# A scan followed by a mixture of adapters: from per-batch phases to one pipeline over units of 512 tokens, with 2 KB runs and part of the gating on GpSimd

## The chip, the cores and the metric

The kernel runs on one core of a Trainium2 chip. The metric is device time in microseconds (us); lower is better. Every run quoted gave the correct result. PE is the matmul engine (PEld its weight loads), DVE is VectorE, ACT is ScalarE, POOL is GpSimd, and SP is the engine that only issues transfers. GB/s is what the core's 16 DMA engines moved. L12 is line 12 of the kernel that the trace belongs to.

## The reference

```
a, b: (8 batches, 6400 steps, 128 channels) fp32
h[t] = a[t] * h[t-1] + b[t]            # per batch and channel, h starts at 0
x = all h as (51200 tokens, 128)
logits = x @ w_gate                    # 8 experts
top 2 experts of each token, weights = softmax over those two
out = x + sum over the two: weight * (x @ A[e]) @ B[e]     # rank 16
```

The two inputs are 26.2 MB each, and so is the output: 78.6 MB of transfers.

## The kernel before

Time runs along the free dimension in the scan, so tokens are transposed in: PE transposes 128x128 fp32 blocks of `a` and `b` into PSUM, ACT copies the transposed `a` to SBUF, and DVE scans 512 tokens at once into `xT` (fp16). Then come logits, gating, `Z = x A`, the gated multiply `zw` on DVE, its transpose, a copy on ACT, the delta matmuls (with `x` added through an identity), the copy out on ACT, and the store.

```
# loads: a whole batch of a, then of b; a run in DRAM is one token, 512 B
sp.dma_start(a_tm[slot][:, :, :], a[bi].rearrange("(j p) d -> p j d", p=128))
sp.dma_start(b_tm[slot][:, :, :], b[bi].rearrange("(j p) d -> p j d", p=128))

# stores, on GpSimd's queue, 512 B runs
pool.dma_start(out[r0:r1, :].rearrange("(j p) d -> p j d", p=128), outt[...])

# order on DVE for each batch k: scans of batch k+1 alternate with multiplies of batch k,
# then the gating of the whole next batch at once
for ci in range(NCH):
    emit_scan(bA, ci + 1); emit_Zw(bZ, ci)
emit_scan(nA, 0); emit_scan(nA, 1)
emit_gating(bA)     # ten dependent DVE operations on 128x400, two sigmoids on ACT between
... (cut)
```

## Time and profile before

| | before |
|---|---|
| time, median of the first 3 runs | 304.25 us (304.02 to 305.71) |
| PE, DVE, ACT busy | 74%, 74%, 57% |
| first scan starts | 28.5 us |
| 512 tokens when fed (128 to 137 us) | 1.88 us on PE, 1.77 us on DVE |
| one batch (78.6 MB / 8 = 9.83 MB of traffic), mid-run | 31.2 us |

The page of the profile has one line of totals, then one digit for each fortieth of the span (busy tenths; 9 means 90% or more), then the GB/s of each fortieth.

```profile
PE 224.9 (74%) x2800; PEld 208.9 (69%) x2800; DVE 224.5 (74%) x290; ACT 172.4 (57%) x330; POOL 80.7 (27%) x113
...
PE   0014993599959996899599877988599859974871
...
DVE  0001892899879987998889787988799889968430
...
DMA  6999999998599989997999889998999641444364
GB/s 194 269 291 289 290 292 290 289 291 252 158 360 327 326 287 353 336 300 238 331 351 292 308 253 353 310 345 241 353 315 342 197 121 37 141 144 117 106 203 125
```

In order: the totals, then PE, DVE, the DMA engines and GB/s by slices. No engine is full, and the holes in PE and DVE recur with a period: one per batch. The timeline of DVE shows such a border (start, length, engine, line, operation, and in brackets the idle time before it and what ended it):

```profile
146.52 1.28 DVE L437 TENSOR_TENSOR_SCAN xT<-a_st,xT,pqB 128x512 f16<-128x512 f32 x1
...
148.03 0.58 DVE L449 COPY L<-pL 128x400 f32<-128x400 f32 x1 [0.23 <-PE pL L248]
...
151.56 0.21 DVE L487 TENSOR_TENSOR d<-m 128x50 f32<-128x50 f32 x1
153.39 0.57 DVE L491 TENSOR_TENSOR t<-mask,w 128x400 f32<-128x400 f32 x1 [1.62 <-ACT w L360]
...
155.15 0.69 DVE L526 TENSOR_TENSOR zw<-pZ,g 128x512 f16<-128x512 f32 x1
```

The lines shown are the last scan before the border, the first and the last step of the gating before the sigmoids, the first step after them, and the first multiply of the next batch. From 147.8 us, when the last scan before it ends, until 155.15 us, when the first multiply of the next batch begins, DVE works at gating, or waits for ACT. Part of that wait comes from the stores: in ACT's order the sigmoid stands behind copies out, two of which had waited for a store just before (1.47 us until 149.25 us, 1.25 us until 151.35 us). At the border near 247 us, where no copy waited for a store, DVE waited 0.45 us for the sigmoid instead of 1.62. Counting from first multiply to first multiply, 123.95 to 155.15 us, a batch takes 31.2 us, of which its 12.5 pairs of scan and multiply need 12.5 x 1.77 = 22 us.

The waits list gives who waited for whom: us in total, number of times, longest.

```profile
DVE xT L437 <- PE pqB L231: 24.1, 5, 17.2
...
ACT outt L378 <- DMA out_dram<-outt: 22.9, 16, 2.9
```

### The profile page before, as it was taken

How to read it: one execution, taken by the hardware profiler on the slowest of the kernel's cores; microseconds unless marked ns; L12 is line 12 of the kernel's file. 1: busy time of each engine (PE TensorE's matmuls, PEld its weight loads, DVE VectorE, ACT ScalarE, POOL GpSimd, SP SyncE). 2: the span in 40 equal slices, each digit the busy share in tenths (PEclk: the TensorE clock that was granted, in tenths of full speed). 3: DMA queues.
4: the chain of work that ended last, by engine and by line, in shares of the span. 5: the costliest groups of instructions: out<-in, count | busy, mean ns of one | idle time of the engine just before them, and what ended most of it. 6: DMA issues, size and time to landing. Idle time of an engine off the chain costs nothing.

```text
span 304.2 us, 7139 instructions
## 1 busy us (share of the span) xinstructions
PE 224.9 (74%) x2800; PEld 208.9 (69%) x2800; DVE 224.5 (74%) x290; ACT 172.4 (57%) x330; POOL 80.7 (27%) x113
## 2 busy tenths in 40 slices
PE   0014993599959996899599877988599859974871
PEld 0003773599949994799499767978589849964760
DVE  0001892899879987998889787988799889968430
ACT  1000430358855784487538673868277946882772
POOL 3000000004430243033312341234213431442452
PEclk9999997769998999699969995999799998995898
DMA  6999999998599989997999889998999641444364
GB/s 194 269 291 289 290 292 290 289 291 252 158 360 327 326 287 353 336 300 238 331 351 292 308 253 353 310 345 241 353 315 342 197 121 37 141 144 117 106 203 125
DMA packets 34048, 79.23 MB, mean 260 GB/s; under 512 B 1984, under 2 KB 1984, under 8 KB 34016
## 3 DMA queue, kind: packets, MB, share of 16 engines
q1 hardware_dynamic: 25856, 52.43, 58.7%
q0 software_dynamic: 8160, 26.36, 26.4%
q8 instruction: 22, 0.36, 0.5%
q14 instruction: 10, 0.08, 0.1%
HBM read 52.56 MB, written 26.21 MB: 259 GB/s over the span
## 4 chain that ended last, share of the span: by engine, by line
DMA 40%; PE 32%; SPq 8%; DVE 8%; ACT 6%; issue 4%; POOL 0%; ACTq 0%; DVEq 0%
DMA out_dram<-outt 21%; DMA b_tm<-in_b_dram 19%; PE pqB L231 7%; PE pqA L215 7%; ACT outt L378 5%; PE pO L293 5%; SPq L145 4%; PE pZ L263 4%; PE pT L277 4%; SPq L149 4%; PE pO L300 4%; DVE xT L437 1%; PE pL L248 1%; DVE g L506 1%; DVE t L491 1%
## 5 line engine op out<-in xcount | busy, mean ns | idle before, releaser
L185 POOL DMA_DIRECT2D out_dram<-outt x104 | 77.9, 749 | 218.5 <-ACT outt L378 213.8
L437 DVE TENSOR_TENSOR_SCAN xT<-a_st,xT,pqB 128x512 f16<-128x512 f32 x96 | 118.0, 1229 | 7.2 <-ACT a_st L353 3.4
L353 ACT COPY a_st<-pqA 128x512 f32<-128x512 f32 (+1 forms) x104 | 59.4, 571 | 67.2 <-PE pqA L215 62.2
L215 PE MATMUL pqA<-ident_f,a_tm 128*128 128x128 f32 x400 | 70.9, 304 | 22.4 <-DMA a_tm<-in_a_dram 16.0
L231 PE MATMUL pqB<-ident_f,b_tm 128*128 128x128 f32 x400 | 69.8, 301 | 16.3 <-DMA b_tm<-in_b_dram 15.6
L378 ACT COPY outt<-pO 128x512 f32<-128x512 f32 (+1 forms) x104 | 59.7, 574 | 32.9 <-DMA out_dram<-outt 22.9
L293 PE MATMUL pO<-cst_h,zwT 128*128 128x128 f16 x400 | 57.0, 222 | 28.6 <-ACT outt L378 27.8
L526 DVE TENSOR_TENSOR zw<-pZ,g 128x512 f16<-128x512 f32 (+1 forms) x104 | 67.7, 652 | 13.5 <-PE pZ L263 12.7
L369 ACT COPY zwT<-pT 128x512 f16<-128x512 f16 (+1 forms) x104 | 59.4, 571 | 20.3 <-PE pT L277 19.1
L231 PEld LDWEIGHTS pqB<-ident_f,b_tm 128*128 128x128 f32 x400 | 53.3, 157 | 19.9 <-DMA b_tm<-in_b_dram 16.5
L215 PEld LDWEIGHTS pqA<-ident_f,a_tm 128*128 128x128 f32 x400 | 48.5, 158 | 24.5 <-issue 16.0
L293 PEld LDWEIGHTS pO<-cst_h,zwT 128*128 128x128 f16 x400 | 39.1, 99 | 34.5 <-issue 34.4
L300 PE MATMUL pO<-ident_h,xT 128*128 128x128 f16 x400 | 57.3, 222 | 0.0
L263 PE MATMUL pZ<-cst_h,xT 128*128 128x128 f16 x400 | 44.1, 238 | 4.3 <-DVE zw L526 4.2
L277 PE MATMUL pT<-ident_h,zw 128*128 128x128 f16 x400 | 40.4, 223 | 2.3 <-ACT zwT L369 2.3
L300 PEld LDWEIGHTS pO<-ident_h,xT 128*128 128x128 f16 x400 | 39.5, 99 | 0.0
L263 PEld LDWEIGHTS pZ<-cst_h,xT 128*128 128x128 f16 x400 | 30.9, 108 | 6.1 <-DVE zw L526 5.6
L277 PEld LDWEIGHTS pT<-ident_h,zw 128*128 128x128 f16 x400 | 24.7, 99 | 3.6 <-issue 2.8
L437 DVE TENSOR_TENSOR_SCAN xT<-a_st,pqB 128x512 f16<-128x512 f32 x8 | 9.7, 1212 | 22.5 <-PE pqB L231 22.5
L248 PEld LDWEIGHTS pL<-cst_h,xT 128*128 128x128 f16 x400 | 24.1, 98 | 1.2
L248 PE MATMUL pL<-cst_h,xT 128*128 128x8 f16 x400 | 24.0, 167 | 0.0
L491 DVE TENSOR_TENSOR t<-mask,w 128x400 f32<-128x400 f32 x8 | 4.6, 575 | 10.2 <-ACT w L360 10.2
(24 smaller groups left out, 48.2 us busy)
## 6 DMA issues: line engine op xcount, KB each, us to landing
out_dram<-outt POOLq DMA_DIRECT2D x96, 256.0 KB, 5.7
out_dram<-outt POOLq DMA_DIRECT2D x8, 128.0 KB, 5.9
a_tm<-in_a_dram SPq DMA_DIRECT2D x8, 0.5 KB, 18.4
b_tm<-in_b_dram SPq DMA_DIRECT2D x8, 0.5 KB, 30.6
cst_f<-in_moe_A_dram POOLq DMA_DIRECT2D x1, 64.0 KB, 7.7
cst_f<-in_moe_B_dram POOLq DMA_DIRECT2D x1, 64.0 KB, 7.5
cst_f<-in_moe_w_gate_dram POOLq DMA_DIRECT2D x1, 4.0 KB, 6.6
```

The source lines that it names most:

```text
L185: pool.dma_start(out[r0:r1, :].rearrange("(j p) d -> p j d", p=128), outt[slot2][:, 0:nb, :],).then_inc(s_od[slot2], 16)
L215: last = pe.transpose(pqA[:, l * 128 : (l + 1) * 128], a_tm[slot][:, jstart + l, :], ident_f[:, :],)
L231: last = pe.transpose(pqB[cg % 2][:, l * 128 : (l + 1) * 128], b_tm[slot][:, jstart + l, :], ident_f[:, :],)
L263: last2 = pe.matmul(pZ[cz % 2][:, q * 128 : (q + 1) * 128], xTb[:, jj * 128 : (jj + 1) * 128], Acat_h,)
L277: last2 = pe.transpose(pT[:, q * 128 : (q + 1) * 128], zw[cz % 3][:, q, :], ident_h[:, :],)
L293: pe.matmul(pO[:, q * 128 : (q + 1) * 128], zwT[cz % 3][:, q * 128 : (q + 1) * 128], Bcat_h, start=True, stop=False,)
L300: last2 = pe.matmul(pO[:, q * 128 : (q + 1) * 128], xTb[:, jj * 128 : (jj + 1) * 128], ident_h[:, :], start=False, stop=True,)
L353: act.copy(a_st[cg % 2][:, 0:w], pqA[:, 0:w]).then_inc(s_aev, 1)
L369: act.copy(zwT[cz % 3][:, 0 : nb * 128], pT[:, 0 : nb * 128]).then_inc(s_zwe, 1)
L378: act.copy(outt[cz % 4][:, 0:nb, :], pO[:, 0 : nb * 128].rearrange("p (q d) -> p q d", q=nb),).then_inc(s_oev, 1)
L437: dve.tensor_tensor_scan(out=xTb[:, cs : cs + w], data0=a_st[cg % 2][:, 0:w], data1=pqB[cg % 2][:, 0:w], initial=init, op0=ALU.mult, op1=A ...
L526: dve.tensor_tensor(out=oview, in0=zview, in1=gview, op=ALU.mult).then_inc(s_zw, 1)
```

## The change

The kernel becomes one stream of 100 units of 512 tokens that takes no notice of batch borders (the scan restarts inside a unit where a batch begins). Each unit's partition row holds four consecutive tokens, so that a run in DRAM is 2 KB. Loads arrive in pieces of 1, 1, 2, 4, 4, ... units in rings of 24 units. Gating goes in groups of four units: the logit copy and one sigmoid on ACT, two maxima on DVE, seven elementwise operations on GpSimd. Stores move from GpSimd's queue to SP's.

```diff
-                    a[bi].rearrange("(j p) d -> p j d", p=128),
+    Q = 4;  UT = 128 * Q;  RING = 24;  G = 4;  LAG = G + 4;  OU = 2;  NOUT = 4
+                        rows[u0 * UT : (u0 + n) * UT, :].rearrange(
+                            "(n p i) d -> p n (i d)", p=128, i=Q)
...
+                view = dst[:, :].rearrange("d (p i) -> d i p", i=Q)   # transposes write PSUM with a 16-byte step
...
+        for s in range(-1, NU + LAG + 3):
+            v = s - LAG
+            if ok(v): z_mm(v)
+            if ok(s + 1): transposes("A", s + 1); a_evac(s + 1)
+            if ok(v - 1): zw_tr(v - 1); t_evac(v - 1)
+            if ok(s + 1): transposes("B", s + 1)
+            if ok(v - 2): delta(v - 2); o_evac(v - 2); (every second unit) store((v - 2) // OU)
+            if ok(s - 1): logits(s - 1); (every fourth) l_evac((s - 1) // G)
+            if ok(s): scan(s)
+            (group c, at s = 4c + 5): gate_m1 on DVE, gate1: 3 operations on GpSimd
+            (group c, at s = 4c + 6): gate_m2 on DVE, gate2: 4 operations on GpSimd, gate_sig on ACT
+            if ok(v): z_mul(v)
+            (loads of the next piece on SP)
```

Each engine executes its own operations in the order of this loop.

## The prediction

> **What bounds it now.** Stages, not one engine (page: DVE and PE 74% busy). The scan's list shows the first scan starting at 28.5 us (a whole batch of a and b must land) and the timeline a wait near 50 us for batch 1 of b. When fed (128-137 us) PE runs back to back, 1.88 us per 512 tokens (two fp32 transpose groups at 0.44, Z 0.22, logits 0.10, zw transposes 0.22, delta 0.44); DVE would need 1.77 (scan plus multiply). Each batch border costs 7-9 us: ten dependent 128x400 gating steps (52.1 us of DVE work in all) plus the sigmoids, while PE idles and its clock drops (transposes then take 0.85 per four). ACT waits 22.9 us for output slots, because stores share DMA engines with bulk loads (busy share about 1.0). Load-only windows move 290 GB/s with 512 B runs.
>
> **What the change does.**
> - Loads arrive in 0.25-1 MB pieces with 2 KB runs. At 290 GB/s 512 B costs one engine 28 ns; the Trainium skill, "DMA: Bandwidth & Descriptors" (Specifications), gives 435 GB/s for the fabric, 18.8 ns, leaving 9.5 ns per run. Estimate for 2 KB: 85 ns, 385 GB/s. The 78.6 MB then need about 204 us.
> - First scan at about 9 us (behind the constants' cast, now 10.9).
> - DVE per unit: 1.77 plus half a 128x128 reduce (0.24, estimated from 0.57 for 400 columns), 1.89. PE: 1.88, always warm. ACT: three copies at 0.48 spacing plus a quarter of (logit copy + sigmoid), 1.6.
> - Gating leaves DVE, but ACT's sigmoid stands in order behind four GpSimd operations. From memset 0.20 and affine select 0.28 I estimate 0.25-0.4 each, 1.6 us with semaphores. ACT should stall 1-1.5 us every fourth unit; part reaches PE and DVE, about 0.6 us. Step: about 2.05 us.
> - New hazard: stores move to the loads' queue. 36 units of load are issued before the first store; the same page (Queues, rings and completion order) says an engine consumes a ring in order, so the store should land only after them, near 52 us. Unit 8's output copy needs that slot at about 40 us: one ACT stall of roughly 10 us, with DMA busy.
>
> **Sum.** Start 9 + ten filling steps at 1.4 (14) + about 89 full steps at 2.05 (182) + one store stall (10) + ten draining steps at 1.4 (14; now 1.38) + last store and rounding (6) = 235 us. DMA alone would allow about 220. Nearly all is on the critical path: start 19, last gating and drain 17, inner borders about 30 net.
>
> **Prediction: 235 us, 8 in 10 between 212 and 268.** Faster by over 2%: 0.92; within 2%: 0.03; slower: 0.05.
>
> **What would show it.** First scan near 9 us; DMA mean near 350 GB/s, load-only about 385; steady spacing of scans 1.9-2.2; PE clock near 1.0 in mid-run; waits list: sigmoid on GpSimd (about 25 times over 1 us) and one long ACT wait for the store at 38-53 us.
>
> **What would break it.** (1) The transposes now write PSUM with a 16-byte step; the skill ("PSUM — Partial Sum Buffer", Specifications) says non-contiguous patterns slow matmuls significantly. I assume the [...]fp32 transposes (0.11 us each, against 0.055 for fp16) hide it; if they doubled, steps would be 2.8 us and nothing gained. This trace has no strided output. (2) 2 KB runs gaining less: at 320 GB/s, DMA-bound at about 260. (3) GpSimd slower than estimated: a longer stall. (4) No store stall: 225.

## More of the kernel before

The windows view of the 162 us in the middle (busy time per engine, clock, mean DMA busy share, GB/s):

```profile
78.00:240.00 162.00, 137.95 (x1813) 130.75 (x1811) 141.68 (x184) 108.86 (x212) 50.52 (x68) 0.92 0.97 308
```

The DMA engines are 97% busy there at 308 GB/s. At that rate a batch's 9.83 MB need 31.9 us, against the 31.2 us that a batch takes.

## The result and the profile after

The changed kernel took 245.12 us (median of 4 runs, 244.71 to 245.75) against 304.13 us (302.38 to 305.71). The ratio is 0.806 (95% interval 0.802 to 0.810). Ratios here are the mean time of one kernel's fast runs over that of the other's of the same rounds, so not quite the ratio of the medians quoted. All timed runs of this document were fast, but for one of the four of e10_runs512_store_pool (slow, left out of its ratio) and the single run of e5_z_strided (unknown). All outputs are right.

```profile
PE 208.9 (86%) x2800; PEld 195.4 (80%) x2800; DVE 193.4 (79%) x257; ACT 172.5 (71%) x352; POOL 87.9 (36%) x181
...
PE   3766989867899999999999999999999999997592
...
DVE  0755988946889888988998898889889888987430
...
GB/s 200 387 387 389 383 387 386 387 392 396 402 396 399 392 400 401 395 400 396 400 395 391 360 386 386 343 405 350 342 404 330 104 134 128 156 108 105 156 175 172
```

The periodic holes are gone, the start is earlier, and the load-only phase moves 383 to 389 GB/s instead of 290. Mid-run, after the start has settled:

```profile
58.00:190.00 132.00, 123.48 (x1744) 117.73 (x1741) 119.17 (x159) 105.41 (x218) 55.70 (x112) 1.00 1.02 382
```

PE is busy 123.5 of 132 us and its clock is full; before it was 0.92 in mid-run. The scans now come in a pattern that repeats every 8.46 us per four units, 2.11 us per unit. Which loop makes this pattern, the chain of waits shows (start, length, engine, tile and line; "issue" is time without a visible wait):

```profile
92.21 1.19 DVE xT L267
93.41 0.30 DVE m_0 L347
...
93.77 0.41 POOL d_0 L358
...
94.27 0.65 POOL pn L365
...
94.99 0.47 POOL d_0 L372
...
95.53 0.47 POOL um L379
...
96.02 0.02 ACT g L390
...
96.24 0.58 ACT a_st L249
...
96.86 0.66 PE pA L237 x4
```

Scan, second maximum on DVE, four GpSimd operations (0.41, 0.65, 0.47, 0.47 us), sigmoid, copy of `a`, transposes; then `b`'s transposes, a multiply and a scan. The sigmoid itself is short. It stands in ACT's order in front of the copy of `a` that the scan after next needs, so all of ACT waits for GpSimd. The waits list:

```profile
ACT g L390 <- POOL um L379: 34.8, 24, 2.6
DVE xT L267 <- ACT a_st L249: 21.2, 23, 2.8
...
ACT outt L454 <- DMA out_dram<-outt: 6.0, 2, 3.5
```

The last line is the predicted late store. It is at one place, 46 to 57 us. SP's timeline and ACT's show how it comes about:

```profile
34.46 2.58 SPq L218 DMA_DIRECT2D b_in<-in_b_dram  x1
37.09 2.56 SPq L463 DMA_DIRECT2D out_dram<-outt  x1
```

```profile
50.02 0.59 ACT L454 COPY outt<-pO 128x512 f32<-128x512 f32 x1 [3.48 <-DMA out_dram<-outt]
...
56.71 0.59 ACT L454 COPY outt<-pO 128x512 f32<-128x512 f32 x1 [2.51 <-DMA out_dram<-outt]
```

SP needs 0.4 to 0.6 us to issue each of the first nine loads, and then mostly about 2.6 us for one of 1 MB: the issue itself is held up once several are under way. The first store's data were ready at 33.3 us, but the store comes behind the loads in SP's order, is issued at 37.1 us, and has landed only at 49.9 us, 1.0 us after the load issued just before it. Then unit 8's copy can go on.

### The profile page after: what moved, and what is told of

Its sections match the earlier page's. It is cut to its first block, busy times and chain, and to the rows that moved or that the text cites. A ratio compares the mean times of both kernels' runs of the same rounds, so it can differ in the third digit from the quotient of the medians.

```text
span 243.7 us, 6924 instructions
## 1 busy us (share of the span) xinstructions
PE 208.9 (86%) x2800; PEld 195.4 (80%) x2800; DVE 193.4 (79%) x257; ACT 172.5 (71%) x352; POOL 87.9 (36%) x181
## 4 chain that ended last, share of the span: by engine, by line
PE 32%; POOL 21%; DVE 20%; DMA 10%; ACT 8%; issue 6%; SPq 1%; POOLq 0%; DVEq 0%; ACTq 0%
DVE xT L267 12%; PE pA L237 10%; PE pB L237 8%; POOL pn L365 6%; DMA out_dram<-outt 5%; ACT a_st L249 5%; PE pT L421 5%; DVE zw L412 5%; DMA b_in<-in_b_dram 4%; POOL um L379 4%; PE pO L440 3%; PE pO L443 3%; PE pZ L398 2%; POOL d_0 L372 2%; POOL d_1 L372 2%
## 5 line engine op out<-in xcount | busy, mean ns | idle before, releaser
L267 DVE TENSOR_TENSOR_SCAN xT<-a_st,xT,pB 128x512 f16<-128x512 f32 x96 | 120.2, 1252 | 26.8 <-ACT a_st L249 21.2
L237 PE MATMUL pA<-ident_f,a_in 128*128 128x128 f32 x400 | 64.7, 286 | 18.5 <-ACT a_st L249 13.6
L249 ACT COPY a_st<-pA 128x512 f32<-128x512 f32 x100 | 58.8, 588 | 19.4 <-PE pA L237 18.4
L412 DVE TENSOR_TENSOR zw<-pZ,g 128x512 f16<-128x512 f32 x100 | 67.4, 675 | 5.1 <-PE pZ L398 3.2
L454 ACT COPY outt<-pO 128x512 f32<-128x512 f32 x100 | 58.9, 589 | 9.9 <-DMA out_dram<-outt 6.0
L237 PE MATMUL pB<-ident_f,b_in 128*128 128x128 f32 x400 | 62.8, 281 | 2.3 <-DMA b_in<-in_b_dram 2.3
L237 PEld LDWEIGHTS pA<-ident_f,a_in 128*128 128x128 f32 x400 | 43.8, 145 | 22.9 <-ACT a_st L249 16.8
L431 ACT COPY zwT<-pT 128x512 f16<-128x512 f16 x100 | 59.6, 596 | 1.0 <-PE pT L421 0.8
L237 PEld LDWEIGHTS pB<-ident_f,b_in 128*128 128x128 f32 x400 | 44.0, 145 | 3.4 <-DMA b_in<-in_b_dram 3.2
L323 POOL TENSOR_TENSOR d_0<-Lg,m_0 128x128 f32<-128x128 f32 x13 | 5.3, 408 | 71.5 <-DVE m_0 L312 71.5
L323 POOL TENSOR_TENSOR d_1<-Lg,m_1 128x128 f32<-128x128 f32 x12 | 4.9, 407 | 49.8 <-DVE m_1 L312 49.8
```

The lines of the kernel that those rows point to most:

```text
L237: last = h.transpose(view[:, i, :], ring[:, w % RING, i * 128 : (i + 1) * 128], ident_f[:, :],)
L249: lambda h: h.copy(a_st[w % 2][:, :], pA[:, :]),
L267: last = h.tensor_tensor_scan(out=xT[:, x0 + lo : x0 + hi], data0=a_st[w % 2][:, lo:hi], data1=pB[w % 2][:, lo:hi], initial=init, op0=ALU. ...
L412: lambda h: h.tensor_tensor(out=oview, in0=zview, in1=gview, op=ALU.mult),
L431: lambda h: h.copy(zwT[w % 2][:, :], pT[:, 0:UT]),
L454: lambda h: h.copy(outt[j % NOUT][:, w % OU, :], pO[:, :]),
```

## The experiments

Twelve kernels were run, each timed against the kernel before (three rounds, except where noted). The table is for reference; the ratio is the one to compare, since the runs were made at different times and on different chips.

| run | edit | us, median | ratio to before |
|---|---|---|---|
| changed kernel | | 245.12 | 0.806 |
| e1_sig_late | sigmoid one unit later | 233.18 | 0.768 |
| e2_ring12 | rings of 12 units | 240.96 | 0.793 |
| e7_both | both | 223.64 | 0.737 |
| e8_fine_start | e7 and eight one-unit pieces first | 222.58 | 0.731 |
| e9_sig_store_pool | e1, stores on GpSimd in front of gating | 265.87 | 0.873 |
| e11_store_pool_later | e1, stores on GpSimd behind gating | 225.50 | 0.742 |
| e4_gate_dve | seven gating operations on DVE | 264.95 | 0.869 |
| e5_z_strided | Z written with a 16-byte step | 245.95 (one run) | |
| e3_runs512 | 512 B runs in the changed kernel | 290.59 | 0.958 |
| e12_runs512_best | 512 B runs in e7 | 273.39 | 0.900 |
| e10_runs512_store_pool | e3, stores on GpSimd | 308.59 (three runs) | 1.014 |
| e6_before_runs2k | 2 KB runs in the kernel before | 296.36 | 0.974 |

### The sigmoid's place (e1_sig_late)

```diff
             c = s - G - 2
                 gate_m2(c // G)
                 gate2(c // G)
-                gate_sig(c // G)
+            c = s - G - 3
+            if c >= 0 and c % G == 0 and c // G < NU // G:
+                gate_sig(c // G)
```

> The changed kernel with one edit: the sigmoid of a group is put into ACT's order one unit later, so that ACT does not stand behind the four GpSimd operations (it waits 34.8 us for them in the changed kernel's trace). Theory A (the loop scan, second maximum, four GpSimd operations, sigmoid, copy of a, transposes, scan sets the pace of 8.46 us per four units): ACT's wait for GpSimd falls below 3 us, the pace falls to DVE's own work of about 7.7 us per four units, and the time to 228 us (226 to 233). Rival B (DMA, 395 GB/s while it loads, is the pace, and the sigmoid's wait only fills slack): the wait goes but the time stays within 1.5% of 245 us, and PE comes to wait for loads instead.

The time fell to 233.2 us, and ACT's wait for GpSimd left the top of the list. So theory A holds for the loop, and B's bound (within 1.5%) is passed. But 5 us of the expected gain are missing, and the waits list says where they are:

```profile
ACT outt L454 <- DMA out_dram<-outt: 16.3, 7, 7.2
```

The wait for stores grew from 6.0 to 16.3 us: a compute side that runs faster meets the store's delay sooner, and seven times instead of twice. The second loss was hidden in part by the first.

### The depth of the load rings (e2_ring12), and both together (e7_both)

```diff
-    RING = 24
+    RING = 12
```

> The changed kernel with the rings of loads cut from 24 to 12 units, nothing else. Theory A (the first stores stand behind the loads that SP has still to issue before them, and behind those in the queue): with at most 12 units of load ahead the first store is issued within 1 us of its copy (37.1 against 33.2 us now), lands in under 6 us, ACT never waits for a store (6.0 us now), and the time falls by about 5 us to 240 us. Rival B (the deep ring is needed to ride out the DMA's shortage in mid-run): PE begins to wait for loads by more than 5 us in all and the time is 245 us or more.

> Both edits: sigmoid one unit later and rings of 12 units. If the two losses are separate and DMA is not yet the limit: 245 - 17 - 5 = 223 us. If DMA becomes the limit once units pass in 7.7 us per four (3.15 MB, 408 GB/s, above the 385 to 400 GB/s seen), PE waits for loads by 5 to 10 us in all and the time is 228 to 233 us, no better than the late sigmoid alone, which has the deeper ring.

With 12 units the first store was issued at 34.2 us, right as its second copy ended, and no wait for a store is left in the list; the time was 241.0 us, and PE's waits for loads stayed as short as before. That first store landed 5.0 us later, within the 6 us expected. The median over all stores stayed at 7.8 us, but no copy had to wait for one. Theory A holds.

Both edits together gave 223.6 us, the 223 us of the plain sum, while the late sigmoid alone had given only 12 of its 17 us. In mid-run everything is now full at once:

```profile
46.00:190.00 144.00, 141.04 (x2030) 137.61 (x2028) 140.17 (x186) 127.24 (x255) 62.71 (x127) 1.00 1.05 397
```

PE is busy 98%, DVE 97%, and the DMA engines move 397 GB/s. e7_both is faster than both kernels.

### A finer start (e8_fine_start)

```diff
-    for n in (1, 1, 2):
+    for n in (1,) * 8:
```

(on top of e7_both, with the semaphores of the first pieces to suit)

> Late sigmoid and rings of 12 as in the best run so far (223.6 us), and the first eight units loaded in pieces of one unit instead of 1, 1, 2, 4. There the fifth scan starts at 16.2 us, 5.9 us after the fourth, waiting for the 1 MB pieces. If that wait is on the path, the fifth scan starts at 12 us and all later work moves up by 3 to 5 us: 219 us (217 to 222). If the DMA total is the limit by now (78.65 MB at 395 GB/s is 199 us), less than 1.5 us is gained.

The fifth scan started 3.8 us earlier, at 12.4 us, as the first case says. But the lead was given back at the ninth, which waits for a 1 MB piece. First e7_both, whose line holds the eighth and the ninth scan (the ninth at 23.1 us), then this run, whose line is the ninth:

```profile
21.66 2.69 DVE L267 TENSOR_TENSOR_SCAN xT<-a_st,xT,pB 128x512 f16<-128x512 f32 x2
```

```profile
21.82 1.28 DVE L267 TENSOR_TENSOR_SCAN xT<-a_st,xT,pB 128x512 f16<-128x512 f32 x1 [3.25 <-PE pB L237]
```

Of the 3.25 us PE itself waited 2.05 us for the load of `b`. The ninth scan came 1.3 us earlier than in e7_both, the tenth 0.9, the last 0.8 (201.5 instead of 202.3 us). The time, 222.6 us, differs by less than 1%, and the intervals of the two ratios overlap. In both kernels the ninth unit needs the first 12 units loaded, and loads ran at 385 and 387 GB/s from 8 to 28 us: the second case of the expectation in its result. That the total of the transfers is the limit to the end is not shown, since PE and DVE are as full in mid-run.

### The stores on another queue (e9_sig_store_pool, e11_store_pool_later)

```diff
-            add("sp", emit, get("oev", j * OU + OU - 1))
+            add("pool", emit, get("oev", j * OU + OU - 1))
```

(late sigmoid, rings of 24; in e11 the store is also emitted one unit later, after the gating operations)

> Late sigmoid with the deep rings of 24 units, and the stores issued by GpSimd on its own queue instead of by SP behind the loads. With SP's order and queue shared, the late sigmoid alone left ACT waiting 16.3 us for stores (233.2 us). Theory A (it is the place behind the loads, in SP's order and queue, that makes the stores late, not the depth of the rings as such): ACT's wait for stores falls below 2 us and the time to 224 us (220 to 228), as with rings of 12. Rival B (outstanding loads delay stores in any queue, since both use the same 16 engines): the wait stays above 8 us and the time above 230 us.

> Late sigmoid, rings of 24, stores on GpSimd's queue, but each store put one unit later in GpSimd's order, behind the gating operations instead of in front of them (in the run with the stores in front, GpSimd stood 75.6 us waiting for output copies and VectorE 45.0 us for the second maximum: 265.9 us, though no wait for a store was left). Theory A (the loads ahead in the shared order and queue make the stores late; the loss in that run was the place in GpSimd's order): ACT's wait for stores below 2 us, VectorE's wait for GpSimd below 5 us, 224 us (220 to 229). Rival B (issuing stores on GpSimd itself delays the gating): VectorE still waits over 15 us for GpSimd and the time is above 235 us.

The first of these was a poor experiment. It removed every wait for a store, as A said, and yet took 265.9 us, as B said, because it added a new wait. GpSimd's timeline:

```profile
101.77 0.73 POOL L463 DMA_DIRECT2D out_dram<-outt  x1 [3.05 <-ACT outt L454]
102.52 0.42 POOL L323 TENSOR_TENSOR d<-Lg,m 128x128 f32<-128x128 f32 x1
```

The store's issue waits 3.05 us for the copy out, and the gating operations stand behind it in GpSimd's order; DVE then waited 45.0 us in all for GpSimd before its second maximum. With the store behind the gating instead (e11), no wait for a store remains, DVE's wait before that maximum is 1.2 us, and the time is 225.5 us with the rings still 24 deep. So it was the place behind the loads, in SP's order and queue, that made stores late, and not the outstanding loads as such. The change's own fault here is the same as the experiment's: an in-order engine that is made to wait for something it need not wait for yet.

### The gating on DVE (e4_gate_dve)

```diff
         gate1, gate2:
-                "pool",
+                "dve",
```

> The changed kernel with the seven elementwise gating operations of a group moved from GpSimd to VectorE, same order. Theory A (VectorE has no room for them, so the move to GpSimd is worth its 2.6 us of latency): seven dependent 128x128 operations at about 0.3 us each, 2.1 us per four units, on top of VectorE's 7.7: 9.6 us per four units against 8.46; 91 units then cost 26 us more, less the store stall that a slower pace avoids: 266 us (257 to 280). Rival B (the chain through GpSimd is so long that doing it on VectorE is no slower, because the loop gets shorter): within 2% of 245 us.

Measured: 264.95 us, as theory A has it. DVE's timeline shows one group of four; the scans repeat every 9.50 us (78.13 to 87.63 us):

```profile
78.13 1.27 DVE L267 TENSOR_TENSOR_SCAN xT<-a_st,xT,pB 128x512 f16<-128x512 f32 x1
...
79.61 0.29 DVE L358 TENSOR_TENSOR d<-Lg,m 128x128 f32<-128x128 f32 x1
79.94 0.23 DVE L365 TENSOR_SCALAR pn<-d 128x128 f32<-128x128 f32 x1
80.08 0.28 DVE L372 TENSOR_TENSOR d<-d 128x128 f32<-128x128 f32 x1
80.40 0.29 DVE L379 TENSOR_TENSOR um<-d,pn 128x128 f32<-128x128 f32 x1
...
87.63 1.27 DVE L267 TENSOR_TENSOR_SCAN xT<-a_st,xT,pB 128x512 f16<-128x512 f32 x1
```

On DVE an operation takes 0.23 to 0.29 us instead of GpSimd's 0.41 to 0.65, so the chain gets shorter, but the time is DVE's own, and DVE is nearly full (busy 127.2 of the 130 us from 60 to 190 us). Moving it to GpSimd is worth about 20 us in this pipeline.

### Does a strided PSUM output cost anything? (e5_z_strided)

```diff
-                        pZ[w % 2][:, i * 128 : (i + 1) * 128], x_block(w, i), Acat_h
+                        pZ[w % 2][:, :].rearrange("p (c q) -> p q c", q=Q)[:, i, :], x_block(w, i), Acat_h
```

> A measurement of a disputed cost: the changed kernel with the four fp16 Z matmuls of a unit writing PSUM with a 16-byte step (column = 4 x expert-rank + block) and the multiply reading it so. Theory A (a strided PSUM output costs a matmul a second cycle per column, which the [...]fp32 transposes hide): the Z matmuls' spacing rises from 0.056 us to 0.11 us, four take 0.44 us instead of 0.22. Rival B (a 16-byte step in PSUM costs the PE nothing): spacing stays at 0.056 us. VectorE's multiply reads with the same step: it stays at 0.67 us or shows its own cost.

Changed kernel first, then this run; each line is a group of four matmuls, and the cost is the distance from its start to that of the next line:

```profile
100.59 0.39 PE L398 MATMUL pZ<-cst_h,xT 128*128 128x128 f16 x4
100.81 0.60 PE L237 MATMUL pA<-ident_f,a_in 128*128 128x128 f32 x4
101.26 0.39 PE L421 MATMUL pT<-ident_h,zw 128*128 128x128 f16 x4
```

```profile
99.94 0.60 PE L398 MATMUL pZ<-cst_h,xT 128*128 128x128 f16 x4
100.33 0.64 PE L237 MATMUL pA<-ident_f,a_in 128*128 128x128 f32 x4
100.81 0.39 PE L421 MATMUL pT<-ident_h,zw 128*128 128x128 f16 x4
```

Four fp16 Z matmuls took 0.22 us with a contiguous output and 0.39 us with the 16-byte step. That is not yet the whole cost: the group behind them takes 0.48 instead of 0.45 us, so a part of it falls behind that group's first start. Within the group the starts of two Z matmuls lie 0.056 us apart without the step and 0.109 us with it (medians, 60 to 160 us). So theory A is right, in size too: nearly twice the time. The fp32 transposes of the changed kernel have the step as well and take 0.45 us for four, 0.109 us apart, as they did without it (0.44 us, before and in e3_runs512). That their longer time hides the step is an inference from these facts. DVE's multiply read the step at no cost (median 0.680 against 0.679 us). The run's time, one look, did not move. The distances of PE's groups (medians) sum to 1.91 us per unit before and 2.12 us after, just the loop's 2.11: PE was now busy in all of the 100 us from 60 to 160 us, instead of 93.5.

### The run length (e3_runs512, e12_runs512_best, e10_runs512_store_pool)

```diff
-                            "(n p i) d -> p n (i d)", p=128, i=Q
+                            "(m p) d -> p m d", p=128
-                view = dst[:, :].rearrange("d (p i) -> d i p", i=Q)
+                view = dst[:, :].rearrange("d (i p) -> d i p", i=Q)
```

(stores and the reads of `xT` alike)

> The changed kernel with the tokens of a unit laid out as before (token = 128 x block + partition): runs of 512 B in loads and stores, transposes writing contiguous PSUM, everything else as in the changed kernel. Theory A (the 2 KB runs carry the DMA rate and the uniform pipeline needs it): load-only rate back to 290 GB/s, about 330 to 350 GB/s with stores mixed in, DMA the limit until the last load; 78.6 MB at 330 gives 238 us plus start and drain: 262 us (252 to 285). Rival B (run length hardly matters, the rings hide it): within 2% of 245 us. The transposes' spacing on PE tells apart whether the 16-byte step in PSUM costs anything: four fp32 transposes at 0.44 us in both if it is hidden.

> The run with 512 B runs (290.6 us) with both repairs that took the changed kernel from 245 to 223.6 us, late sigmoid and rings of 12. Theory A (with 512 B runs DMA alone sets the pace at 309 GB/s: 78.65 MB need 254 us, and what the engines do better is not seen): 280 to 291 us, mid-run rate unchanged at 305 to 315 GB/s. Rival B (the repairs are worth their 21 us whatever the run length): 265 to 272 us.

> The run with 512 B runs (290.6 us, 10.2 us per four units, 308 GB/s in mid-run) with its stores moved to GpSimd's queue, as the kernel before has them, which moved up to 353 GB/s in mid-run with the same run length. Theory A (two queues let loads and stores of 512 B overlap better): mid-run 340 to 355 GB/s, 9.1 us per four units, 267 us (260 to 277). Rival B (the rate is set by the run length alone; the kernel before only showed short windows): 300 to 315 GB/s and 284 to 293 us.

With 512 B runs the pipeline alone gave 290.6 us, 4% better than before and above the range expected. Mid-run DMA is full at 309 GB/s; then, after the last load, comes a long end at 175 GB/s:

```profile
80.00:230.00 150.00, 118.43 (x1652) 107.34 (x1651) 113.61 (x150) 95.67 (x207) 50.24 (x102) 1.00 1.07 309
230.00:270.00 40.00, 34.73 (x498) 31.91 (x496) 33.73 (x46) 30.01 (x64) 15.75 (x32) 1.00 0.62 175
```

With the late sigmoid and rings of 12 (e12) the rate in mid-run stayed, but the time fell by 17 us, to 273.4 us:

```profile
80.00:230.00 150.00, 125.97 (x1672) 121.55 (x1673) 115.95 (x152) 103.52 (x208) 50.66 (x103) 0.92 1.07 310
230.00:270.00 40.00, 28.97 (x396) 25.68 (x393) 23.03 (x32) 26.59 (x53) 11.83 (x24) 0.93 0.82 234
```

So both theories of that run were off. The rate is the run length's, as A said (310 GB/s), and the loads are what PE now waits for:

```profile
PE pB L237 <- DMA b_in<-in_b_dram: 38.3, 25, 2.7
```

But 24 units of loads that run ahead leave their stores to the end, where little else moves. In e3, when the last load had landed (235.0 us), 33 of the 50 stores had landed too, and 53.3 us were still to come; in e12 (243.2 us) it was 39 stores and 26.7 us. The changed kernel and e7_both, with 2 KB runs, have the same 33 and 39, so the count goes with the depth of the rings. How the 17 us divide between the rings and the late sigmoid, which speeds up the end as well, was not tested. A full DMA in mid-run does not make order irrelevant: what counts is also how much work is left when the loads are done.

e10 asked whether two queues let 512 B traffic overlap better. The rate was 314 GB/s from 80 to 230 us, with the DMA engines' busy share at 1.01, so they do not, or hardly; the 353 GB/s of the kernel before were short windows in an average of 308. Its 308.6 us (against the kernel before 1.014, interval 1.008 to 1.021, so slower, though not clearly by 2%) are over the range of either theory. The waits list points to the fault of e9, though no run took it away here: ACT waited 90.1 us for GpSimd, and GpSimd 119.9 us for the copies out that its stores need.

### The run length alone in the kernel before (e6_before_runs2k)

```diff
+    t_in[bi][0 : NF * 128, :].rearrange("(c p i) d -> p c (i d)", p=128, i=CHB)   # NF = 48 of the 50 blocks
+    t_in[bi][NF * 128 : S, :].rearrange("(p i) d -> p (i d)", p=128)              # the last two
```

(with transposes, `xT` reads and stores to suit; everything else as before)

> The kernel before with 2 KB runs alone: within each chunk of 512 tokens four tokens per partition row (two in the last chunk of 256), loads, transposes and stores changed to suit, no uniform pipeline. If the runs alone carry most of the gain, as the loss in the run with 512 B runs might suggest (290.6 us): 255 us or less. Theory A (with whole-batch loads and a serial gating at each border the faster DMA only shortens the start and the waits for stores): first scan at 22 us instead of 28.5, load-only rate 385 instead of 290 GB/s, ACT's waits for stores from 22.9 to under 10 us, time 282 us (270 to 292).

The expectation was a miss: 296.4 us instead of 282 us. The first scan came at 22.9 us and loads alone ran at 383 GB/s (10 to 38 us), as expected, and the wait for stores fell to 12.9 us, but the time fell by little more than the start. The ratio of 0.974 (0.968 to 0.981) is a gain, though the runs leave open whether it is over 2%. The middle of the run:

```profile
80.00:204.00 124.00, 107.16 (x1410) 102.29 (x1409) 111.41 (x146) 85.05 (x165) 28.10 (x52) 0.94 0.88 326
```

DMA is no longer full (88%, 97% before), and yet batches follow each other at 30.8 us (mean of four, 81.2 to 204.3 us) instead of 31.2. Most of that is the serial gating and the scan pairs themselves, but not all. At each of these borders ACT still waits 2.2 to 3.0 us for a store, in front of the sigmoid:

```profile
198.55 0.58 ACT L387 COPY outt<-pO 128x512 f32<-128x512 f32 x1 [3.00 <-DMA out_dram<-outt]
```

The batch from 203.7 to 233.0 us, whose border has no such wait, takes 29.3 us (at full clock, 0.94 in the mean of the four). So the engines' own pace with their border is at most 30.8 us, and by this one batch about 29.

This closes the account. In mid-run the kernel before had two limits at nearly one height: DMA at 308 GB/s, 31.9 us per batch, and engines with their border, 29 to 31 us. Lifting the DMA's alone gives 2.6%. Lifting the engines' alone gives 4.2% (e3), or 10% with the repaired order (e12). Lifting both gives 19%, or 26% repaired (e7). And e12's 10% does not come from the middle: from the first scan to the last it takes 242.8 us, the kernel before 239.2, e7 195.9. What e12 gains lies before the first scan (7.1 instead of 28.5 us) and after the last (19.9 instead of 36.5 us).

## Why the prediction was right, and where its terms were off

The time, 245 us, lies in the range of 212 to 268 us, 10 us above the 235 us forecast. That it is so near is in part luck: in the table below three terms came out 18.5 us too long together and three 9.7 us too short. The trace of the changed kernel (span 243.7 us) has the terms of the sum:

| term | predicted, us | measured, us | from |
|---|---|---|---|
| start to the first scan | 9 | 6.6 | scan's first start |
| filling | 14 | 17.3 | first scan 6.6 to the ninth, 23.9 (eight steps, ten were forecast) |
| full steps | 89 x 2.05 = 182 | 91 x 2.11 = 192 | ninth scan to the last, 221.1, less the stall |
| store stall | 10 | 5.3 | three scan steps at 46.7 to 58.3 us, less 3 x 2.11 |
| draining | 14 | 19.2 | last scan to the last store's issue, 240.3 |
| last store and rounding | 6 | 3.4 | to the end of the span |

- **The step.** The mechanism was named: DVE and PE at 1.9 us, and ACT's sigmoid behind GpSimd costing the rest. e1_sig_late shows it, by taking it away. The size was a little off, 2.11 instead of 2.05 us. GpSimd was slower than estimated: the compare-and-scale operation took 0.65 us and the others 0.41 to 0.46 us, where 0.25 to 0.4 us was forecast. ACT's stand was still 1.45 us on average, 24 times, within the forecast 1 to 1.5 us, so what was too small is the part of it that reaches DVE: 8.46 us less four times the forecast 1.89 us leaves 0.9 us per four units, not 0.6.
- **DMA.** The load-only estimate of 385 GB/s, from 512 B traffic and the fabric's figure that the prediction cites, met 383 to 389 GB/s. The mean over the span was 325 GB/s, not 350, because the run was longer.
- **The store.** It was named, with its place (38 to 53 us forecast, 46 to 57 us seen) and its cause, which e2_ring12 and e11_store_pool_later show. The prediction put it down to the order within a ring, and the trace fits that: the store landed 1.0 us after the load issued just before it. It adds that SP itself is held while issuing, so part of the queue is SP's program. No run tells the two apart. The size was 5 us, not 10, since the copy of unit 8 came later than estimated.
- **Filling and draining** were 8.5 us short together. The fill waits for the first 1 MB pieces (smaller ones help little, see e8_fine_start), and the drain has the last group's gating on its path (ACT waits 2.25 us for GpSimd once more there).
- **PSUM.** The risk was real, as e5_z_strided shows for fp16, and the assumption held that fp32 transposes do not feel it.
- **The step that was wrong** is one of attribution: "Nearly all is on the critical path: start 19, last gating and drain 17, inner borders about 30 net". As a list of savings this adds up to a number near the truth, but it treats the inner borders as gained by the pipeline. e12_runs512_best shows that the inner borders are not gained by the pipeline alone (242.8 us from the first scan to the last, 239.2 before), and e6_before_runs2k that the faster DMA alone gains little.

What stays open: why the 16-byte step costs fp16 matmuls 0.053 us each, and how far below 222 us the kernel could go. In e7_both PE, DVE and DMA are all within 3% of full in mid-run, so further gains there need less work, not a better order.

## What to carry to other kernels

Before valuing a change that lifts one limit, compute the pace of each of the others in the same stage (here 9.83 MB at 308 GB/s, 31.9 us, beside a border-bound batch of 29 to 31 us); two limits at nearly one height yield only together. In an in-order engine, put an operation behind everything that does not need it: a sigmoid moved by one place in the order was worth 12 us, and 17 us once the stores were out of the way. Prefetch only as deep as the stores behind it can bear, or give stores a queue and an order of their own.

## What the Trainium skill lacked or had wrong

- "PSUM — Partial Sum Buffer" (Specifications) says that any non-contiguous access pattern slows matmuls significantly. It gives no size, and no exception: fp16 matmuls of 128 columns went from 0.056 to 0.109 us with a 16-byte step, fp32 transposes stayed at 0.11 us each (0.45 against 0.44 us for four).
- "DMA: Bandwidth & Descriptors" (Specifications) gives 512 B as the least transfer for line rate. Here runs of 512 B were far from it: with pieces of up to 1 MB in both cases, loads alone ran at 291 GB/s with 512 B runs and at 387 GB/s with 2 KB runs, and loads with stores at 309 and 397 GB/s. This concerns that row alone, not all that the skill says of transfer sizes.
- The same page (Issuing engines are not separate DMA queues) says that issuing from several engines saves only the sequencer's time, usually small. Issuing a 1 MB load took SP about 2.6 us once several were under way, against 0.4 to 0.6 us at first, and moving the stores off SP's queue, behind the gating, took 233.2 us to 225.5 us, because they no longer stood behind loads.
- "GPSIMD Engine Reference" (Engine selection) calls one-input elementwise operations on GpSimd roughly line-rate and two-input ones slower. Here the one-input compare-and-scale on 128x128 fp32 took 0.65 us and two-input add and subtract 0.41 to 0.46 us; on DVE the same operations took 0.23 and 0.28 to 0.29 us. The compare-and-scale does two arithmetic steps, and 128 elements per partition are few: whether a rate or a fixed cost makes the 0.65 us was not tested.
